# SwiGLU feed-forward: the first 256 rows of x turned by a transposing DMA copy instead of TensorE

## The chip, the cores and the metric

The kernel runs on one core of a Trainium2 chip. The metric is the device time of one execution in microseconds. Before the change it was 163.65 us, the median of 3 runs (163.2 to 164.01).

## What is computed

```python
B, S, D, F = 1, 2048, 640, 1536        # all tensors bfloat16

def reference(x, w_gate, w_up, w_down):
    g = silu(x @ w_gate)               # [S, F]
    u = x @ w_up                       # [S, F]
    return (g * u) @ w_down            # [S, D]
```

## The kernel before

All operands stay in SBUF. The 2048 rows of x are worked in four blocks of 512 (`S_BLK`). For each block and each of the twelve 128-wide slices `fc` of F, TensorE multiplies five 128x128 weight tiles (`kd`, over D = 640) with the transposed block `xT`, once for the gate (`pg`) and once for the up projection (`pu`). ACT takes silu of `pg` (L214), VectorE multiplies it with `pu` into `aT` (L215). Then the down projection goes over `aT` and `wd_sb` (L261 for the last 128 columns, L291 for the first 512), ACT copies the result out of PSUM and SP stores it. The last four rows are computed on VectorE with products and sums (`row_dots`, L147), spread over the later blocks.

The matmuls need x with D on the partitions. Rows 256 to 2047 are brought in that layout by transposing DMA copies (`turn_x`, L105), all issued from SP. Rows 0 to 255 are loaded as they lie into `x_sb` (`load_x`, L86), one 128-row chunk from SP and one from ACT; TensorE turns them with ten 128x128 transposes against the identity `ident` (`transpose_chunk`, L185), and ACT and VectorE copy the results to `xT` (L190). GpSimd makes the identity.

The start of the kernel is written out by hand. SP's queue has, in this order: the x chunk, four slices of the gate weights (`wg_sb[:, kd, 0:512]`, L115, one for each kd; the one of kd = 1 comes from ACT's queue), the transposing copy of rows 256-511, two slices of the up weights (L83), the larger weight chunks, the down weights (L125), and the transposing copy for block 1. On ACT, the first silu, which brings its table in, stands behind its two DMA issues (L119). `keep_order` holds the order of TensorE, ACT, VectorE and SP as it was traced, so that no scheduler moves these.

`head()` does the first four slices `fc` of block 0. TensorE first does `N_WARM` = 18 matmuls on ones (L176), whose result is not used, then the ten transposes, then gate steps for all four slices with kd outermost: kd = 0 in two halves of 128 columns, kd = 1 to 4 with 256 columns (rows 0-255), and then all kd with the other 256 columns (rows 256-511). The four up projections with 512 columns follow, each with its silu and product. From there on the loops are the plain ones.

Of the kernel before, what the change touches and what calls it, by code (L numbers as in the profile page):

```python
# [7 lines left out]


@with_exitstack  # L10
def _body(
# [8 lines left out]
    nc = tc.nc  # L20
    P = nc.NUM_PARTITIONS
    f32 = mybir.dt.float32
    bf16 = mybir.dt.bfloat16
    ACT = mybir.ActivationFunctionType
    ALU = mybir.AluOpType

    B, S0, D = x.shape
    F = w_gate.shape[1]
    S = B * S0
    x2 = x.rearrange("b s d -> (b s) d")  # L30
    out2 = out.rearrange("b s d -> (b s) d")

    KD = D // P
# [4 lines left out]
    HALF = S_BLK // 2  # L38
    DA = 512
    Q = 32  # L40
    N_WARM = 18
    T = 4
    WT_STEP = 4
    ROW_J = 0
    EARLY = 4
# [3 lines left out]
    consts = ctx.enter_context(tc.tile_pool(name="consts", bufs=1))  # L49
    work = ctx.enter_context(tc.tile_pool(name="work", bufs=3))  # L50
    outp = ctx.enter_context(tc.tile_pool(name="outp", bufs=3))
    psum = ctx.enter_context(
        tc.tile_pool(name="psum", bufs=2, space=bass.MemoryType.PSUM)
    )

    ident = consts.tile([P, P], bf16)
    x_sb = consts.tile([P, HALF // P, D], bf16)
    xT = consts.tile([P, KD, S], bf16)
    wg_sb = consts.tile([P, KD, F], bf16)
    wu_sb = consts.tile([P, KD, F], bf16)  # L60
# [7 lines left out]
    row_s = consts.tile([P, KF, T], f32)  # L68
    prod = consts.tile([P, D], f32)

    make_identity(nc, ident[:])

    x_v = x2.rearrange("(c p) d -> p c d", p=P)
    xt_v = x2.rearrange("s (kd p) -> s kd p", p=P)
    wg_v = w_gate.rearrange("(kd p) f -> p kd f", p=P)
    wu_v = w_up.rearrange("(kd p) f -> p kd f", p=P)
# [2 lines left out]
    def wslice(a, b):  # L79
        return slice(a * P, b * P)  # L80

    def load_w(eng, dst, src, a, b):
        eng.dma_start(out=dst[:, :, wslice(a, b)], in_=src[:, :, wslice(a, b)])  # L83

    def load_x(eng, c0, c1):
        eng.dma_start(out=x_sb[:, c0:c1, :], in_=x_v[:, c0:c1, :])  # L86

    def issue_order(a, b):
        tc.add_manual_dep(
# [8 lines left out]
    def keep_order(engine):  # L98

        traced = [i for i in nc.cur_bb.bb.instructions if i.engine == engine]  # L100
        for a, b in zip(traced, traced[1:]):
            issue_order(a, b)

    def turn_x(r0, r1):
        nc.sync.dma_start_transpose(out=xT[:, :, r0:r1], in_=xt_v[r0:r1])  # L105

    ones = consts.tile([P, P], bf16)
    silu_first = consts.tile([P, 1], f32)
    nc.vector.memset(ones[:], 1.0)  # L109

    load_x(nc.sync, 0, 1)
    load_x(nc.scalar, 1, 2)
    for kd in range(KD):
        eng = nc.scalar if kd == 1 else nc.sync
        eng.dma_start(  # L115
            out=wg_sb[:, kd, wslice(0, EARLY)], in_=wg_v[:, kd, wslice(0, EARLY)]
        )
    turn_x(HALF, S_BLK)
    nc.scalar.activation(silu_first[:], ones[:, 0:1], ACT.Silu)  # L119
    for a in range(0, EARLY, 2):  # L120
        load_w(nc.sync, wu_sb, wu_v, a, a + 2)
    for a, b in W_CHUNKS:
# [6 lines left out]
    def turn_w(dst, src, f0, f1):  # L129
# [7 lines left out]
        out=x_row[:],  # L137
        in_=x2[S - T : S, :].rearrange("t d -> (t d)").partition_broadcast(P),
# [35 lines left out]
    def warm(n):  # L174
        for _ in range(n):
            nc.tensor.matmul(  # L176
                pw[:, 0:P], lhsT=ones[:], rhs=ones[:], start=True, stop=True
            )

    def transpose_chunk(c, parts):  # L180
        c_sl = slice(c * P, (c + 1) * P)
        for copy, tag, k0, k1 in parts:
            pt = psum.tile([P, k1 - k0, P], bf16, tag=tag, name="pt")
            for kd in range(k0, k1):
                nc.tensor.transpose(  # L185
                    out=pt[:, kd - k0, :],
                    in_=x_sb[:, c, kd * P : (kd + 1) * P],
                    identity=ident[:],
                )
            copy(out=xT[:, k0:k1, c_sl], in_=pt[:])  # L190

    def proj_step(ps, w_sb, fc, sb, c0, c1, kd):
        nc.tensor.matmul(  # L193
            ps[:, c0:c1],
            lhsT=w_sb[:, kd, fc * P : (fc + 1) * P],
            rhs=xT[:, kd, sb * S_BLK + c0 : sb * S_BLK + c1],
            start=(kd == 0 and c0 in (0, HALF)),
            stop=(kd == KD - 1),
        )

    def proj(ps, w_sb, fc, sb, c0, c1):
        for kd in range(KD):
            proj_step(ps, w_sb, fc, sb, c0, c1, kd)
# [6 lines left out]
    def gate(pg, pu, sb, fc, n_s):  # L210

        s0 = sb * S_BLK
        sg = work.tile([P, S_BLK], f32, name="sg")
        nc.scalar.activation(sg[:, 0:n_s], pg[:, 0:n_s], ACT.Silu)  # L214
        nc.vector.tensor_tensor(  # L215
            out=aT[:, fc, s0 : s0 + n_s], in0=sg[:, 0:n_s], in1=pu[:, 0:n_s], op=ALU.mult
        )

    def head():
        dve, act = nc.vector.tensor_copy, nc.scalar.copy  # L220
        split = [(act, "po_a", 0, 2), (dve, "po_b", 2, KD)]
        pgs = [
            psum.tile([P, S_BLK], f32, tag="gu", name="pg", bufs=4)
            for _ in range(EARLY)
        ]
        warm(N_WARM)
        for c in range(HALF // P):
            transpose_chunk(c, split)

        steps = [(0, 0, P), (0, P, HALF)]  # L230
        steps += [(kd, 0, HALF) for kd in range(1, KD)]
        steps += [(kd, HALF, S_BLK) for kd in range(KD)]
        for kd, c0, c1 in steps:
            for fc in range(EARLY):
                proj_step(pgs[fc], wg_sb, fc, 0, c0, c1, kd)

        for fc in range(EARLY):
            pu = psum.tile([P, S_BLK], f32, tag=("po_a", "po_b")[fc % 2], name="pu")
            proj(pu, wu_sb, fc, 0, 0, S_BLK)
            gate(pgs[fc], pu, 0, fc, S_BLK)  # L240
        keep_order(mybir.EngineType.PE)
        keep_order(mybir.EngineType.Activation)

    head()
    for sb in range(NSB):
        n_s = S_BLK if sb < NSB - 1 else S_BLK - T
# [26 lines left out]
        for q in range(P // Q):  # L273
            nc.scalar.dma_start(
                out=out2[
                    sb * S_BLK : sb * S_BLK + n_t, DA + q * Q : DA + (q + 1) * Q
                ].rearrange("(i r) c -> r i c", r=Q),
                in_=ot_q[q * Q : (q + 1) * Q, :].rearrange("r (i c) -> r i c", c=Q),
            )

        for j in range(SUB):
# [6 lines left out]
            for c0, c1, tag in cols:  # L288
# [14 lines left out]
                eng = nc.sync if c1 < D else nc.scalar  # L303
# [82 lines left out]
def kernel(tc, *args):  # L386
    _body(tc, *args)
    tc.close()
    tc.compile()
    _trim(tc.nc)  # L390
# [30 lines left out]
```

## Time and profile before

| | |
|---|---|
| time, median of 3 runs | 163.65 us (163.2 to 164.01) |
| span of the profiled execution, first to last instruction | 161.8 us |
| time of the runs above that span | 1.4 to 2.2 us, 1.85 for the median |
| TensorE matmul busy | 159.4 us (99%) |
| VectorE, ACT busy | 111.0 us (69%), 42.6 us (26%) |
| DMA | 15.86 MB, mean 98 GB/s |
| transposing copies of x, from SP | 4 |

The profile is one execution; it gives the span, and the time that the runs show beyond it lies around the span. PE is TensorE's matmul side, PEld its weight load, SPq and ACTq the DMA issues of SP and ACT, L12 a line of the kernel. A matmul's length includes its way through the array, so that lengths of neighbours overlap; the distance between starts is the pace.

### The profile page before, as it was taken

To read this page: it belongs to the slowest core of one execution; us is meant where nothing else is said; L and a number is where in the kernel's file an instruction comes from. 1 tells how busy PE (TensorE), PEld (TensorE's weight loads), DVE (VectorE), ACT (ScalarE), POOL (GpSimd) and SP (SyncE) were. 2 spreads that over 40 slices of the span, in tenths; PEclk is the share of its full clock that TensorE was granted. 3 is DMA by queue.
4 is the path that set the end of the run, shared out by engine and by line. 5 is a ranking of instruction groups with operands and counts; after the bars stand their busy time and mean duration, and the time that the engine had idled before them with its cause. 6 is when DMAs were issued, how large, how long until landed. Compare 5 with 4: busy or idle time off the path is not lost.

```text
span 161.8 us, 2142 instructions
## 1 busy us (share of the span) xinstructions
PE 159.4 (99%) x808; PEld 77.6 (48%) x808; DVE 111.0 (69%) x250; ACT 42.6 (26%) x74; POOL 0.6 (0%) x6
## 2 busy tenths in 40 slices
PE   8999999999999999999999999999999999999995
PEld 7854444444444444444444444444444444445454
DVE  2034223599569999989919999979964999993001
ACT  5051222112222222211222322221214222222121
POOL 1000000000000000000000000000000000000000
PEclk9999999999999999999999999999999999999999
DMA  6999999934189999003110000000321000000312
GB/s 212 231 351 349 361 248 231 222 75 91 34 192 159 235 236 184 4 0 34 65 65 0 0 4 2 0 0 3 62 67 34 0 0 0 0 0 4 48 41 73
DMA packets 41961, 15.86 MB, mean 98 GB/s; under 512 B 33504, under 2 KB 41824, under 8 KB 41952
## 3 DMA queue, kind: packets, MB, share of 16 engines
q1 hardware_dynamic: 33584, 14.93, 37.0%
q10 hardware_dynamic: 8368, 0.80, 3.5%
q8 instruction: 6, 0.10, 0.3%
q14 instruction: 3, 0.02, 0.1%
HBM read 6.88 MB, written 2.62 MB: 59 GB/s over the span
## 4 chain that ended last, share of the span: by engine, by line
PE 97%; DMA 2%; SPq 0%; DVE 0%; issue 0%
PE pg L193 32%; PE pu L193 32%; PE po_a L291 26%; PE po_t L261 6%; DMA wg_sb<-in_w_gate_dram 2%; SPq L86 0%; DVE ot_b L302 0%
## 5 line engine op out<-in xcount | busy, mean ns | idle before, releaser
L193 PE MATMUL pg<-xT,wg_sb 128*128 128x512 bf16 (+3 forms) x264 | 59.8, 363 | 0.1
L193 PE MATMUL pu<-xT,wu_sb 128*128 128x512 bf16 (+1 forms) x240 | 59.1, 379 | 0.0
L215 DVE TENSOR_TENSOR aT<-sg,pu 128x512 bf16<-128x512 f32 (+1 forms) x48 | 32.7, 682 | 32.3 <-PE pu L193 32.3
L214 ACT ACTIVATE sg<-pg 128x512 f32<-128x512 f32 (+1 forms) x48 | 28.4, 597 | 71.2 <-PE pg L193 67.4
L291 PE MATMUL po_a<-wd_sb,aT 128*128 128x512 bf16 (+4 forms) x228 | 42.8, 348 | 0.0
L147 DVE SCALAR_TENSOR_TENSOR prod<-wgT,x_row 128x640 f32<-128x640 bf16 x48 | 39.4, 821 | 1.5 <-DMA wgT<-in_w_gate_dram 0.4
L147 DVE SCALAR_TENSOR_TENSOR prod<-wuT,x_row 128x640 f32<-128x640 bf16 x48 | 39.4, 821 | 1.0
L193 PEld LDWEIGHTS <-wg_sb 128*128 128x128 bf16 x264 | 25.9, 100 | 26.8 <-DMA wg_sb<-in_w_gate_dram 0.4
L193 PEld LDWEIGHTS <-wu_sb 128*128 128x128 bf16 x240 | 23.4, 98 | 28.1 <-DMA wu_sb<-in_w_up_dram 0.3
L291 PEld LDWEIGHTS <-aT 128*128 128x128 bf16 x228 | 20.8, 98 | 21.7
L300 ACT CAST ot<-po_a 128x512 bf16<-128x512 f32 (+2 forms) x17 | 9.5, 559 | 31.8 <-PE po_a L291 20.2
L261 PE MATMUL po_t<-aT,wd_sb 128*128 128x512 bf16 (+1 forms) x48 | 10.4, 366 | 0.0
L261 PEld LDWEIGHTS <-wd_sb 128*128 128x128 bf16 x48 | 4.7, 98 | 5.1
L302 DVE CAST ot_b<-po_a 128x96 bf16<-128x96 f32 (+1 forms) x2 | 0.5, 240 | 9.7 <-PE po_a L291 9.6
L270 ACT CAST ot_t<-po_t 128x512 bf16<-128x512 f32 (+1 forms) x4 | 2.2, 559 | 11.6 <-PE po_t L261 11.6
L147 DVE DVE_READ_ACCUMULATOR prod<-wgT,x_row 128x1 f32 x48 | 3.9, 82 | 0.0
L147 DVE DVE_READ_ACCUMULATOR prod<-wuT,x_row 128x1 f32 x48 | 3.9, 82 | 0.0
L272 DVE STREAM_TRANSPOSE ot_q<-ot_t 128x512 bf16<-128x512 bf16 (+1 forms) x4 | 2.7, 676 | 1.7 <-ACT ot_t L270 1.7
L190 DVE COPY xT<-pt 128x384 bf16<-128x384 bf16 x2 | 0.7, 358 | 2.9 <-PE pt L185 2.9
L176 PE MATMUL pw<-ones 128*128 128x128 bf16 x18 | 2.1, 313 | 0.4 <-DVE ones L109 0.4
L176 PEld LDWEIGHTS <-ones 128*128 128x128 bf16 x18 | 1.8, 147 | 0.4 <-DVE ones L109 0.4
L119 ACT ACT_TABLE_LOAD x1 | 1.3, 1283 | 1.0 <-issue 1.0
(13 smaller groups left out, 4.7 us busy)
## 6 DMA issues: line engine op xcount, KB each, us to landing
wd_sb<-in_w_down_dram SPq DMA_DIRECT2D x1, 1920.0 KB, 13.0
out_dram<-ot SPq DMA_DIRECT2D x15, 128.0 KB, 1.7
wg_sb<-in_w_gate_dram SPq DMA_DIRECT2D x2, 640.0 KB, 7.9
wu_sb<-in_w_up_dram SPq DMA_DIRECT2D x2, 640.0 KB, 8.6
wu_sb<-in_w_up_dram SPq DMA_DIRECT2D x2, 320.0 KB, 4.7
x_row<-in_x_dram SPq DMA_DIRECT2D x1, 640.0 KB, 5.1
wg_sb<-in_w_gate_dram SPq DMA_DIRECT2D x4, 128.0 KB, 3.4
out_dram<-ot_q ACTq DMA_DIRECT2D x12, 32.0 KB, 1.9
```

Of the source, the lines that this page charges most:

```text
L119: nc.scalar.activation(silu_first[:], ones[:, 0:1], ACT.Silu)
L147: nc.vector.scalar_tensor_tensor(out=prod[:], in0=wT[:, fc, :], scalar=1.0, in1=x_row[:, t, :], op0=ALU.mult, op1=ALU.mult, accum_out=acc[ ...
L176: nc.tensor.matmul(pw[:, 0:P], lhsT=ones[:], rhs=ones[:], start=True, stop=True)
L190: copy(out=xT[:, k0:k1, c_sl], in_=pt[:])
L193: nc.tensor.matmul(ps[:, c0:c1], lhsT=w_sb[:, kd, fc * P : (fc + 1) * P], rhs=xT[:, kd, sb * S_BLK + c0 : sb * S_BLK + c1], start=(kd == 0 ...
L214: nc.scalar.activation(sg[:, 0:n_s], pg[:, 0:n_s], ACT.Silu)
L215: nc.vector.tensor_tensor(out=aT[:, fc, s0 : s0 + n_s], in0=sg[:, 0:n_s], in1=pu[:, 0:n_s], op=ALU.mult)
L261: nc.tensor.matmul(po_t[:], lhsT=wd_sb[:, kf, DA:D], rhs=aT[:, kf, sb * S_BLK : sb * S_BLK + n_t], start=(kf == 0), stop=(kf == KF - 1),)
L270: nc.scalar.copy(ot_t[:], po_t[:])
L272: nc.vector.transpose(out=ot_q[:], in_=ot_t[:])
L291: nc.tensor.matmul(po[:], lhsT=aT[:, kf, s0 : s0 + P], rhs=wd_sb[:, kf, c0:c1], start=(kf == 0), stop=(kf == KF - 1),)
L300: nc.scalar.copy(ot[:], po[:])
```

## The change

Rows 0-255 of x come by the same kind of transposing copy as the others, issued from SP as its first DMA. The gate slices follow it on SP's queue as three transfers (kd 0; kd 1-2; kd 3-4), none on ACT's, then the transposing copy of rows 256-511, then all as before. `x_sb`, the identity, the ten transposes and their copies are gone. ACT begins with the first silu. There are 26 warming matmuls instead of 18, and the first gate step (kd = 0) is done in 256 columns at once, like the others.

```diff
-    N_WARM = 18
+    N_WARM = 26
...
-    ident = consts.tile([P, P], bf16)
-    x_sb = consts.tile([P, HALF // P, D], bf16)
...
-    make_identity(nc, ident[:])
...
-    load_x(nc.sync, 0, 1)
-    load_x(nc.scalar, 1, 2)
-    for kd in range(KD):
-        eng = nc.scalar if kd == 1 else nc.sync
+    def load_d(eng, k0, k1):
         eng.dma_start(
-            out=wg_sb[:, kd, wslice(0, EARLY)], in_=wg_v[:, kd, wslice(0, EARLY)]
-        )
+            out=wg_sb[:, k0:k1, wslice(0, EARLY)], in_=wg_v[:, k0:k1, wslice(0, EARLY)]
+        )
+
+    nc.scalar.activation(silu_first[:], ones[:, 0:1], ACT.Silu)
+    turn_x(0, HALF)
+    load_d(nc.sync, 0, 1)
+    load_d(nc.sync, 1, 3)
+    load_d(nc.sync, 3, KD)
     turn_x(HALF, S_BLK)
-    nc.scalar.activation(silu_first[:], ones[:, 0:1], ACT.Silu)
...
-    def transpose_chunk(c, parts):
...
-        dve, act = nc.vector.tensor_copy, nc.scalar.copy
-        split = [(act, "po_a", 0, 2), (dve, "po_b", 2, KD)]
...
         warm(N_WARM)
-        for c in range(HALF // P):
-            transpose_chunk(c, split)
-
-        steps = [(0, 0, P), (0, P, HALF)]
-        steps += [(kd, 0, HALF) for kd in range(1, KD)]
+        steps = [(kd, 0, HALF) for kd in range(KD)]
         steps += [(kd, HALF, S_BLK) for kd in range(KD)]
```

More of the change, by code (lines that the diff above doesn't have):

```diff
@@ L6 @@
 from concourse._compat import with_exitstack
-from concourse.masks import make_identity
 @with_exitstack
@@ L69, in _body @@
     prod = consts.tile([P, D], f32)
-    make_identity(nc, ident[:])
-    x_v = x2.rearrange("(c p) d -> p c d", p=P)
     xt_v = x2.rearrange("s (kd p) -> s kd p", p=P)
@@ L83, in load_w @@
         eng.dma_start(out=dst[:, :, wslice(a, b)], in_=src[:, :, wslice(a, b)])
-    def load_x(eng, c0, c1):
-        eng.dma_start(out=x_sb[:, c0:c1, :], in_=x_v[:, c0:c1, :])
     def issue_order(a, b):
@@ L178, in warm @@
             )
-    def transpose_chunk(c, parts):
[L181 to L188, printed above, removed]
-                )
-            copy(out=xT[:, k0:k1, c_sl], in_=pt[:])
     def proj_step(ps, w_sb, fc, sb, c0, c1, kd):
```

## The prediction

> **What bounds the kernel now.** I read the busy shares first, then the chain of work that ended last, then the first 16 us of the timeline, then the DMA issues with their landings.
>
> ```profile
> span 161.8 us, 2142 instructions
> PE 159.4 (99%) x808; PEld 77.6 (48%) x808; DVE 111.0 (69%) x250; ACT 42.6 (26%) x74; POOL 0.6 (0%) x6
> PE 97%; DMA 2%; SPq 0%; DVE 0%; issue 0%
> ```
>
> TensorE is the bound, and 97% of the chain is its matmuls. The chain in order of time (start, us, what) shows the only part that is not:
>
> ```profile
> 0.45 3.21 DMA wg_sb<-in_w_gate_dram
> 3.71 5.21 PE pg L193 x44
> 8.92 4.37 PE pu L193 x20
> 13.29 1.08 PE pg L193 x5
> ...
> 30.55 2.59 PE po_t L261 x12
> ```
>
> From 8.92 on, every five 512-column matmuls take 1.08 us without a gap, up to the end. Nothing behind the first up-projection changes in this edit, so the whole question is when that first pu matmul starts. A shift there goes to the end one for one, unless a load further on is late too.
>
> ```profile
> 0.00 0.39 SPq L86 DMA_DIRECT2D x_sb<-in_x_dram  x1
> ...
> 0.39 2.10 PE L176 MATMUL pw<-ones 128*128 128x128 bf16 x18 [0.39 <-DVE ones L109]
> 0.45 1.84 SPq L115 DMA_DIRECT2D wg_sb<-in_w_gate_dram  x4
> ...
> 2.31 1.25 PE L185 MATMUL pt<-ident,x_sb 128*128 128x128 bf16 x10
> ...
> 2.33 1.91 SPq L105 DMA_TRANSPOSE xT<-in_x_dram  x1
> ...
> 4.29 1.15 SPq L83 DMA_DIRECT2D wu_sb<-in_w_up_dram  x2
> ...
> 8.63 1.57 ACT L214 ACTIVATE sg<-pg 128x512 f32<-128x512 f32 x3 [4.98 <-PE pg L193]
> ...
> 8.79 4.49 PE L193 MATMUL pu<-xT,wu_sb 128*128 128x512 bf16 x20
> ```
>
> The columns are start, length, engine, line. SP's issues stand back to back: 0.46 us for each gate slice (1.84 over 4), 1.91 us for one transposing copy of 256 rows, 0.58 us for each up slice. How long from issue to landing, in the first 7 us (KB each, median us), and for the first up slice alone:
>
> ```profile
> wg_sb<-in_w_gate_dram SPq DMA_DIRECT2D x4, 128.0 KB, 3.4
> x_sb<-in_x_dram SPq DMA_DIRECT2D x1, 160.0 KB, 2.3
> xT<-in_x_dram SPq DMA_TRANSPOSE x1, 4.2
> ```
>
> ```profile
> L83 SPq DMA_DIRECT2D wu_sb<-in_w_up_dram x1: 583/583/583, 4.3 to 4.3; - x1
> DMA to landing us min/median/max: 4.5/4.5/4.5
> ```
>
> The transposed rows 256-511 land at 2.33 + 4.2 = 6.53, the first up slice at 4.29 + 4.5 = 8.79. That is exactly the start of pu. So **two transfers set the head, both on the edge**: behind 6.53 stand twenty 256-column matmuls of the second half, and pu follows 2.26 us after that landing (8.79 - 6.53); the up slice lands 2.26 us after it as well.
>
> **The change, part by part.**
>
> *TensorE.* Ten transposes (1.25 us) and their two pairs of copies go, eight warming matmuls come: 2.10 / 18 = 0.117 us each with the last one's tail, 0.107 between starts, so the warming ends near 0.39 + 26 x 0.107 = 3.2. The first eight 128-column matmuls become four of 256 columns, the same columns. All this is before the data is there, worth nothing by itself. The identity on GpSimd and the table load moved ahead on ACT are worth nothing too: ACT's first sigmoid-linear work is at 8.63.
>
> *SP's issues.* Now the queue holds: transposing copy 1 at 0.0 for 1.91; three gate transfers, the first 0.46, the two double ones between 0.46 and the 0.58 of the five-slice up load, say 0.52; then transposing copy 2. It is issued at 1.96 + 0.46 + 2 x 0.52 = 3.46, against 2.33: **1.13 us later**. The ACT queue, which carried one x chunk and one gate slice, helps no more. If copy 2 again lands 4.2 us after its issue, it lands at 7.66, +1.13: the upper bound of this chain.
>
> *The transfers themselves.* The other end comes from bytes. These are windows of the trace (busy times, then granted clock, DMA share, GB/s), and a 512-row copy, issued at 44.6 into a nearly empty queue:
>
> ```profile
> 5.10:5.80 0.70, 0.70 (x9) 0.63 (x7) 0.00 (x0) 0.00 (x0) 0.00 (x0) 1.00 1.27 275
> 5.80:6.80 1.00, 1.00 (x11) 0.81 (x10) 0.00 (x0) 0.00 (x0) 0.00 (x0) 1.00 0.52 118
> 6.80:8.80 2.00, 2.00 (x21) 1.66 (x18) 0.00 (x0) 0.17 (x1) 0.00 (x0) 1.00 1.01 308
> 45.80:46.90 1.10, 1.10 (x7) 0.50 (x6) 1.10 (x2) 0.12 (x1) 0.00 (x0) 1.00 0.87 159
> 46.90:48.50 1.60, 1.60 (x9) 0.69 (x7) 1.56 (x5) 0.47 (x1) 0.00 (x0) 1.00 1.27 286
> ```
>
> ```profile
> L105 SPq DMA_TRANSPOSE xT<-in_x_dram x1: 2732/2732/2732, 44.6 to 44.6; - x1
> DMA to landing us min/median/max: 5.4/5.4/5.4
> ```
>
> That copy began to move bytes at about 45.8, 1.2 us after its issue, went at 159 GB/s for 1.1 us and then at 286. Copy 1 is 328 kB: 1.2 + 1.1 us for the first 175 kB, 0.53 us for the other 153, so it is drained near 2.85 and lands some 0.65 later (as copy 2 now does: drained by 5.85, landed 6.53), at 3.5. Its price beside the two plain x loads is small in bytes and large in what follows: after the transposing copy of the trace, from 5.8 to 6.8, the engines moved 118 GB/s where 308 was to be had, 0.62 us lost. Now that dip comes twice, the first time ahead of the gate slices. Gate slices: 2.85 + 0.62 + 655 kB at 308 (2.1) = 5.6. Copy 2 at 286: 1.15, drained at 6.7; landing 0.65 later, **7.35, +0.8**. Without a dip behind copy 1 it would be 6.7, +0.2; that is the lower bound. I take **+0.85**, between the two chains (+0.8 by bytes, +1.13 by issue) and next to the one by bytes, since SP's 1.91 may be shorter where no earlier transfer fills the queue (half of the 2.73 for 512 rows is 1.37, which takes 0.54 off the issue chain).
>
> In the Trainium skill, Advanced Engine Details and Errata, X-Bar Transpose (TRN2), transposing copies are as fast as plain ones, 350 to 400 GB/s. The windows above differ: 159 and then 286 GB/s, and the measurement decides; by the page's figure copy 1 would drain about 0.7 us sooner and the sum would be near +0.15.
>
> *The first gate matmuls* wait for copy 1 (3.5) and for gate slice 0, which stands behind it: 2.85 + 0.62 + 131 kB at 308 (0.43) + about 0.5 to land = 4.4 (bounds: 1.96 + 2.3 = 4.3 by the quick x load, 1.96 + 3.4 = 5.4 by the slow gate loads). So TensorE starts pg 0.7 us later than 3.71 and idles 1.2 us instead of 0.4. The first half, 20 matmuls of 256 columns, needs 2.2 us at the pace of the second half and so ends at 6.6 to 6.9, ahead of 7.4: hidden, as long as the pace is that. If it is not, see the clock below.
>
> *The up slices* follow copy 2 on the queue, 2.26 us behind its landing as now, so they come when pu wants them. The load one chunk further has this much room:
>
> ```profile
> 10.11 1.67 SPq L125 DMA_DIRECT2D wd_sb<-in_w_down_dram  x1
> ...
> 14.06 0.89 PEld L193 LDWEIGHTS <-wu_sb 128*128 128x128 bf16 x5 [0.19 <-DMA wu_sb<-in_w_up_dram]
> 14.20 1.24 PE L193 MATMUL pu<-xT,wu_sb 128*128 128x512 bf16 x5
> ```
>
> ```profile
> wd_sb<-in_w_down_dram SPq DMA_DIRECT2D x1, 1920.0 KB, 13.0
> ```
>
> Between the weight load and its matmul stand 0.14 us. If the stream moves by 1.13 and TensorE by 0.85, 0.14 more is lost there; the range has it. The down weights land at 23.1 and are first used at 30.55, so they have room.
>
> **Sum:** 161.8 + 0.85 = 162.65 of span. The runs of before lie 1.4 to 2.2 us above that span (163.2 to 164.01), 1.85 for the median, so 164.5 against 163.65.
>
> **Rivals.**
>
> *The clock (slower still).* The granted-clock column says 1.00 from the start, but the spacing says otherwise:
>
> ```profile
> 3.71 0.72 PE L193 MATMUL pg<-xT,wg_sb 128*128 128x128 bf16 x5
> 6.27 2.65 PE L193 MATMUL pg<-xT,wg_sb 128*128 128x256 bf16 x22
> 1.54:4.95 3.41, 3.26 (x29) 2.81 (x28) 0.72 (x2) 1.71 (x4) 0.00 (x0) 1.00 0.96 287
> ```
>
> 128 columns took (0.72 - 0.29) / 4 = 0.107 us until then; later 256 columns take (2.65 - 0.27) / 21 = 0.113, a stall included. TensorE ran at half speed up to about 4.95, 4.5 us of almost unbroken work. Now the work breaks off from 3.2 to 4.4. If the count starts anew there, the whole first half runs at 0.214 each, 4.4 + 4.3 = 8.7, the second takes 2.2 and a little more: pu at 11.0, +2.2. If it changes at 7.0: 12 done by then, 8 at 0.11, 7.9 + 2.2 = 10.1, +1.3. So 165.0 to 165.9, middle 165.4. For it: the break, and that a faster TensorE would starve between gate slices. Against: the trace has a break of 0.4 us in its stretch and still got full speed at 4.95. The Trainium skill, TensorE: Matmul & The Clock Gate, Part 1, has a free-running window of about 3.4 us which must be busy; an estimate from it: a warming of 2.8 us does not fill one, which speaks against this change. The trace's 3.26 busy of 3.41 agrees with it but does not show how much idleness is allowed.
>
> *Hidden anyway (no change).* No dip behind copy 1, SP's issue 1.37: copy 2 lands at 6.7, +0.2, 163.85. For it: two issues fewer on ACT's queue, whose packets shared the same engines. Against: the 118 GB/s.
>
> *Faster.* The gate slices now have one queue, and the first copy drains before them. If copy 1 is through by 2.6 and the slices need only 1.87 us (350 GB/s), copy 2 drains at 5.6 and lands at 6.25, and pu starts 0.3 us sooner: 163.35. It decides in favour when copy 2 lands ahead of 6.53. Against: copy 2 cannot be issued before 2.9 even with 1.37 for the first, and every dip must be gone.
>
> That the change does not do what it says is out: the instruction order has the two transposing copies first and fifth on SP and no transposes on TensorE.
>
> **How the numbers follow.** A measurement of this kernel tells about 0.5% (0.82 us) from no change. Forecast 164.5 (164.2 to 164.8): 0.48, of which 0.29 lies over 164.47. Clock: 0.27, all slower. Hidden: 0.18, same. Faster: 0.07, of which 0.05 is allowed beyond 0.5%. Slower 0.29 + 0.27 = 0.56, same 0.39, faster 0.05. The range goes from 163.5, which takes in most of the hidden case, to 165.9, the end of the clock's; it leaves out the faster case and the lower edge of the hidden one, under 2 in 10.
>
> **What would show it.** In the changed profile: copy 1 issued at 0.0 for 1.4 to 1.9 us and landing near 3.5; pg's first matmul near 4.4 with a wait of over 1 us on a gate slice, not on xT; copy 2 issued near 3.5, landing near 7.4; a low-rate stretch after each copy; pu at 9.65; from there the same 1.08 us steps. Wrong if pu starts under 9.0 (the dip or the issue was overpriced), or over 10, with 256-column matmuls 0.214 apart beyond 6 us (the clock).

## The result and the profile after

| | before | after |
|---|---|---|
| time, median of 6 runs | 163.64 us | 165.58 us (164.74 to 165.86) |
| ratio after / before | | 1.0118, 95% interval 1.0096 to 1.0141 |
| span of the profiled execution | 161.8 us | 164.5 us (a run of 165.86 us) |

The change costs 1.94 us, at the median. The two profiled executions differ by 2.7 us, since that of before was one of the quick ones: this run of after lies 1.36 us above its span, and the profiled runs below lie 1.3 above theirs, so a span of 161.8 belongs to some 163.15 us, not to the median.

The chain of work that ended last, in order of time, for the first 18 us of the kernel after (start, us, what):

```profile
0.00 1.34 SPq L96
1.34 0.06 issue
1.39 0.56 SPq L103
1.96 0.05 issue
2.01 3.88 DMA wg_sb<-in_w_gate_dram
5.89 0.05 issue
5.93 5.77 PE pg L174 x36
11.70 0.05 issue
11.76 4.26 PE pu L174 x19
```

The DMA piece is the second gate transfer (kd 1-2), which stands behind slice 0 on the queue: it landed at 2.01 + 3.88 = 5.89, and 36 of the 40 gate matmuls come behind it. The gate matmuls end, by their modelled ends, at 11.70 instead of 8.92. (The record of the first pu matmul is missing; 19 of 20 are there. Before, it started 0.13 us ahead of that modelled end, which puts it near 11.55 here, against 8.79.) Behind them the steps are the old 1.08 us. The timeline of the same execution:

```profile
0.39 2.96 PE L169 MATMUL pw<-ones 128*128 128x128 bf16 x26 [0.39 <-DVE ones L100]
1.39 1.55 SPq L103 DMA_DIRECT2D wg_sb<-in_w_gate_dram  x3
2.98 2.28 SPq L96 DMA_TRANSPOSE xT<-in_x_dram  x1
5.22 6.49 PE L174 MATMUL pg<-xT,wg_sb 128*128 128x256 bf16 x40 [1.87 <-DMA wg_sb<-in_w_gate_dram]
```

TensorE stands idle from the end of its warming to 5.22, and what it waits for is a gate slice, not x; behind the first four gate matmuls comes a second, shorter break, up to 5.93. Issue and landing of the first copy (L96), the first gate slice (L103) and the second copy (L96):

```profile
L96 SPq DMA_TRANSPOSE xT<-in_x_dram x1: 1336/1336/1336, 0.0 to 0.0; - x1
DMA to landing us min/median/max: 3.7/3.7/3.7
...
L103 SPq DMA_DIRECT2D wg_sb<-in_w_gate_dram x1: 563/563/563, 1.4 to 1.4; - x1
DMA to landing us min/median/max: 3.8/3.8/3.8
...
L96 SPq DMA_TRANSPOSE xT<-in_x_dram x1: 2279/2279/2279, 3.0 to 3.0; - x1
DMA to landing us min/median/max: 4.9/4.9/4.9
```

Copy 1 lands at 3.7, gate slice 0 at 1.39 + 3.8 = 5.2, copy 2 at 2.98 + 4.9 = 7.9. That is 1.36 later than before, and if that were all, pu would start 2.26 behind it, at 10.1. It starts near 11.55. The rest is in the granted clock. These are four stretches of the kernel after (busy times by engine; the last three columns are granted clock, DMA share, GB/s):

```profile
0.39:3.33 2.94, 2.94 (x26) 2.69 (x26) 0.00 (x0) 1.22 (x2) 0.04 (x2) 1.00 0.61 128
3.33:6.74 3.41, 1.43 (x13) 1.04 (x13) 0.00 (x0) 0.00 (x0) 0.00 (x0) 1.00 1.03 245
6.74:10.15 3.41, 3.41 (x19) 2.43 (x17) 0.00 (x0) 0.00 (x0) 0.00 (x0) 0.50 1.06 274
10.15:11.54 1.39, 1.39 (x14) 1.25 (x13) 0.00 (x0) 0.13 (x1) 0.00 (x0) 1.00 1.04 344
```

The clock column reads 1.00 until the first change that was recorded, at 3.33; the 26 warming matmuls before it are 0.107 us apart, which the prediction showed to be half the pace. From 3.33 on the full clock was granted. TensorE was busy for 1.43 us of the stretch 3.33 to 6.74, and in the next one, of the same 3.41 us, it was granted half the clock. Its matmuls, in the timeline by shape:

```profile
6.71 3.58 PE L174 MATMUL pg<-xT,wg_sb 128*128 128x256 bf16 x16
```

Sixteen in 3.58 us with the last one's tail, over 0.2 us apart where 0.11 is the full pace. The full clock had come early, while there was nothing to multiply; twelve gate matmuls ran at it, and then it was gone for the next sixteen. The Trainium skill, TensorE: Matmul & The Clock Gate, Part 1, tells of a free-running window of about 3.4 us and of two clocks, full and half; the stretches of this trace agree (3.41, 1.00 and 0.50). It lets the clock fall after an idle window; here a stretch with 1.43 us of work was idle enough, and the measurement decides. Where the stretches fall is not the same in every execution: e3 below has the same warming and a like break, and its clock rose at 8.70, so that its gate began at half speed.

### The profile page after: what moved, and what is told of

Read it like the earlier page. It is cut to its first block, busy times and chain, and to the rows that moved or that the text cites. A ratio compares the mean times of both kernels' runs of the same rounds, so it can differ in the third digit from the quotient of the medians.

```text
span 164.5 us, 2106 instructions
## 1 busy us (share of the span) xinstructions
PE 159.7 (97%) x790; PEld 77.8 (47%) x802; DVE 110.4 (67%) x248; ACT 41.9 (25%) x72; POOL 0.2 (0%) x4
## 4 chain that ended last, share of the span: by engine, by line
PE 95%; DMA 2%; SPq 1%; issue 0%; DVE 0%
PE pg L174 32%; PE pu L174 31%; PE po_a L266 26%; PE po_t L236 6%; DMA wg_sb<-in_w_gate_dram 2%; SPq L96 1%; SPq L103 0%; DVE ot_b L277 0%
## 5 line engine op out<-in xcount | busy, mean ns | idle before, releaser
L174 PE MATMUL pg<-xT,wg_sb 128*128 128x512 bf16 (+2 forms) x254 | 60.6, 371 | 2.3 <-DMA wg_sb<-in_w_gate_dram 1.9
L169 PE MATMUL pw<-ones 128*128 128x128 bf16 x26 | 3.0, 313 | 0.4 <-DVE ones L100 0.4
L169 PEld LDWEIGHTS <-ones 128*128 128x128 bf16 x26 | 2.7, 148 | 0.4 <-DVE ones L100 0.4
```

The source lines that it names most:

```text
L169: nc.tensor.matmul(pw[:, 0:P], lhsT=ones[:], rhs=ones[:], start=True, stop=True)
L174: nc.tensor.matmul(ps[:, c0:c1], lhsT=w_sb[:, kd, fc * P : (fc + 1) * P], rhs=xT[:, kd, sb * S_BLK + c0 : sb * S_BLK + c1], start=(kd == 0 ...
```

## Experiments

Ratios are to the kernel before on the same chip, with 95% intervals. Two theories: the **clock theory**, that the break in TensorE's work costs most of what copy 2's landing does not explain; and the **transfer theory**, that the late landings alone make the 1.9 us. Then, what makes the landings late.

### Longer warming (e1), hardly any (e9)

```diff
-    N_WARM = 26
+    N_WARM = 60      # e9: 1
```

> The changed kernel with 60 warming matmuls instead of 26, so that TensorE is busy until the first gate slice lands near 5.2. Clock theory (the break from 3.2 to 5.2 lets TensorE fall back to half speed from 6.7 to 10.2, worth some 1.4 us in the profiled run): no half-speed stretch behind 5.5, time near 164.5 to 164.9, 0.7 to 1.1 us under the changed kernel's 165.6 and 0.9 to 1.3 over before. Transfer theory (the late landings alone make the 1.9 us): no change, 165.6. If the longer warming itself delays the first gate matmul by more than the break, over 165.6.

> The changed kernel with 1 warming matmul instead of 26, so that TensorE is all but idle until the first gate slice lands near 5.2. If the loss is a matter of stretches of 3.4 us, each of which grants the next one its speed by how busy it was, the warming buys a full-speed stretch while TensorE has nothing to do: without it the gate runs at half speed from 5.2 to somewhere between 7 and 11, and the time is 165.2 to 166.4, no better and on the mean no worse than 165.6. If the warming itself caused the drop by coming too early: under 165.0. Transfer theory: 165.6 unchanged.

Measured: 60 matmuls 164.72 us (1.0066, 1.0044 to 1.0087), 26 are the change itself (1.0118), 1 gives 165.74 us (1.0149, 1.0124 to 1.0174). The same stretches with 60, and the gate's rows in the timelines of both, first 60, then 1:

```profile
3.33:6.74 3.41, 3.41 (x46) 3.30 (x44) 0.00 (x0) 0.00 (x0) 0.00 (x0) 1.00 1.01 247
6.74:10.15 3.41, 3.41 (x32) 2.97 (x31) 0.00 (x0) 0.19 (x1) 0.00 (x0) 1.00 1.11 279
```

```profile
5.63 4.63 PE L174 MATMUL pg<-xT,wg_sb 128*128 128x256 bf16 x40
```

```profile
4.74 7.47 PE L174 MATMUL pg<-xT,wg_sb 128*128 128x256 bf16 x40 [4.05 <-DMA wg_sb<-in_w_gate_dram]
```

With 60 there is no break and the 40 matmuls take 4.63 us, although they begin 0.4 later than in the change; without warming they take 7.47. (The clock column is of no use in these two executions, since no change was recorded in them: with 1 warming matmul it reads 1.00 also where the matmuls are 0.21 us apart.) The copies land where they did (copy 2 at 7.9 with 60, at 7.5 with 1). So the transfer theory falls: with 60 the landings stayed and the time fell by 0.85 us, 1.94 to 1.1, with intervals apart. Some 0.85 us is what the longer warming brings back by the clock, and 1.1 is the rest; since 60 warming matmuls ended 0.5 after the gate slice's landing, 1.1 is rather too much for the landings alone, and 0.85 too little for the clock. Whether the 26 were worth anything against 1 is not settled, the intervals of 1.0118 and 1.0149 just overlap.

### No warming in the kernel before (e2)

```diff
-    N_WARM = 18
+    N_WARM = 1
```

> The kernel before with 1 warming matmul instead of 18: no transfer changes, only TensorE's early work is missing until 2.3 us. Clock theory: full speed comes later, the first half of the gate is slower, 0.5 to 1.5 us over before (164.1 to 165.1). Transfer theory: the two transfers at 6.5 and 8.8 set the time whatever the speed is, so no change (within 0.3 us).

Measured: 163.98 us, 1.0017 (0.9995 to 1.0040): no difference that can be told, as the transfer theory had it for this kernel. Its timeline says why:

```profile
2.59 1.25 PE L185 MATMUL pt<-ident,x_sb 128*128 128x128 bf16 x10 [1.91 <-DMA x_sb<-in_x_dram]
3.63 3.19 PE L193 MATMUL pg<-xT,wg_sb 128*128 128x128 bf16 x24
7.12 2.34 PE L193 MATMUL pg<-xT,wg_sb 128*128 128x256 bf16 x20 [0.30 <-DMA xT<-in_x_dram]
```

From 2.59 TensorE has work without a long break, the first half of the gate is done by 6.8, and copy 2 (7.1 in this execution) sets the rest. The kernel before owes its steady work to the early x chunks, not to the warming. It also shows that copy 2's landing varies by half a microsecond between two executions with the same transfers (6.53 and 7.1).

### Gate slices from ACT's queue (e3)

```diff
-    load_d(nc.sync, 0, 1)
-    load_d(nc.sync, 1, 3)
-    load_d(nc.sync, 3, KD)
+    load_d(nc.scalar, 0, 1)
+    load_d(nc.scalar, 1, 3)
+    load_d(nc.scalar, 3, KD)
```

ACT's first silu stands behind the three issues here.

> The changed kernel with the three gate transfers issued from ACT's queue, so that they do not stand behind the first transposing copy and the second copy is issued at about 1.4 instead of 3.0. If the queue order is what makes the gate slices and the second copy late: gate slice 0 lands before 4.2, the second copy before 6.8, time within 0.4 us of before (163.2 to 164.0). If it is the transposing copies themselves (slow stretches, shared engines) and not the order: second copy still near 7.5 and time 164.5 or more.

Measured: 165.72 us, 1.0129 (1.0112 to 1.0145). The two copies (L96), and the stretch in which the gate matmuls begin:

```profile
L96 SPq DMA_TRANSPOSE xT<-in_x_dram x1: 1322/1322/1322, 0.0 to 0.0; - x1
DMA to landing us min/median/max: 5.6/5.6/5.6
...
L96 SPq DMA_TRANSPOSE xT<-in_x_dram x1: 2141/2141/2141, 1.4 to 1.4; - x1
DMA to landing us min/median/max: 6.2/6.2/6.2
```

```profile
5.29:8.70 3.41, 3.03 (x15) 2.17 (x15) 0.00 (x0) 0.00 (x0) 0.00 (x0) 1.00 1.22 252
```

The gate slices no longer stand behind copy 1, and now copy 1 lands at 5.6, with the traffic of the other queue beside it. Copy 2, issued 1.6 us sooner than in the change, lands at 7.6, 0.3 sooner. So its issue time is not what sets its landing. The break in TensorE's work is as long as ever (2.32 us), only it now ends with copy 1, at 5.6, and the first 15 gate matmuls take 3.03 us, 0.2 us each, up to the rise of the clock at 8.70 (until which the clock column reads 1.00).

### A plain copy in the place of the first transposing one (e4, e13)

```diff
-    turn_x(0, HALF)
+    nc.sync.dma_start(
+        out=xT[:, :, 0:HALF],
+        in_=x2[0:HALF].rearrange("(p r) d -> p (r d)", p=P).rearrange(
+            "p (kd s) -> p kd s", s=HALF
+        ),
+    )
```

> The changed kernel with the first transposing copy replaced by a plain copy of the same bytes in the same place of SP's queue; the 256 rows are not transposed, so their results are not the reference's. It prices the crossbar: by the theory that the transposing copy costs a slow start and a slow stretch behind it (1.5 us against 0.9 for its bytes, then 0.6), gate slice 0 lands 0.8 to 1.3 us sooner (3.9 to 4.4), the second copy near 6.9, time 164.0 to 164.6. If the order on one queue is what costs, not the crossbar: gate slice 0 still lands near 5 and the time stays over 165.

e13 is the same with 60 warming matmuls.

> The changed kernel with 60 warming matmuls and a plain copy of the same bytes in the place of the first transposing copy (rows 0-255 are not transposed, so their results are not the reference's). If the crossbar makes what the queue order does not (0.4 us): 164.2 to 164.4. If the place on one queue makes it all: 164.6 to 164.9, as with the transposing copy and long warming.

Measured: e4 165.50 us (1.0092, 1.0067 to 1.0117), e13 164.84 us (1.0065, 1.0042 to 1.0089). Gate slice 0, copy 2 and the later gate matmuls in e4, and the GB/s of e4 where the change has its slow stretch:

```profile
L103 SPq DMA_DIRECT2D wg_sb<-in_w_gate_dram x1: 608/608/608, 0.7 to 0.7; - x1
DMA to landing us min/median/max: 3.3/3.3/3.3
...
L96 SPq DMA_TRANSPOSE xT<-in_x_dram x1: 1807/1807/1807, 2.4 to 2.4; - x1
DMA to landing us min/median/max: 5.7/5.7/5.7
```

```profile
6.02 5.77 PE L179 MATMUL pg<-xT,wg_sb 128*128 128x256 bf16 x36 [1.30 <-DMA wg_sb<-in_w_gate_dram]
```

```profile
3.00:3.50 0.50, 0.35 (x4) 0.08 (x1) 0.00 (x0) 0.00 (x0) 0.00 (x0) 1.00 1.25 228
3.50:4.00 0.50, 0.00 (x0) 0.00 (x0) 0.00 (x0) 0.00 (x0) 0.00 (x0) 1.00 0.61 168
4.00:4.50 0.50, 0.39 (x4) 0.31 (x4) 0.00 (x0) 0.00 (x0) 0.00 (x0) 1.00 0.72 197
4.50:5.00 0.50, 0.22 (x2) 0.00 (x0) 0.00 (x0) 0.00 (x0) 0.00 (x0) 1.00 0.88 258
```

and the same stretches of the change:

```profile
3.00:3.50 0.50, 0.35 (x4) 0.08 (x1) 0.00 (x0) 0.00 (x0) 0.00 (x0) 1.00 0.62 118
3.50:4.00 0.50, 0.00 (x0) 0.00 (x0) 0.00 (x0) 0.00 (x0) 0.00 (x0) 1.00 0.77 176
4.00:4.50 0.50, 0.00 (x0) 0.00 (x0) 0.00 (x0) 0.00 (x0) 0.00 (x0) 1.00 0.91 244
4.50:5.00 0.50, 0.00 (x0) 0.00 (x0) 0.00 (x0) 0.00 (x0) 0.00 (x0) 1.00 1.03 364
```

Half of the expectation came: gate slice 0 lands at 4.05 instead of 5.2. But the engines then move 168 to 258 GB/s without any transposing copy in front, copy 2 is issued 0.6 us sooner and lands at 2.36 + 5.7, near 8.0, not sooner at all. The second gate transfer, through which the chain goes here as in the change, is there at 5.97 instead of 5.89, so the early slice 0 only moves the break behind the first four matmuls. With long warming the plain copy gives 1.0065 against the transposing one's 1.0066, and its copy 2 lands at 8.2. So the transposing in the first copy is not what makes the transfers behind it late; that the place in the queue is, is tried next. (The time of e13 says less than its landings: in its profiled execution the chain went through the 60 warming matmuls, which ended at about 6.2, so a gain of 0.2 us at the landings would not have been seen.)

### Parts of the queue order in the kernel before (e5, e6, e11)

```diff
 # e5: three gate transfers, all from SP
-    for kd in range(KD):
-        eng = nc.scalar if kd == 1 else nc.sync
-        eng.dma_start(
-            out=wg_sb[:, kd, wslice(0, EARLY)], in_=wg_v[:, kd, wslice(0, EARLY)]
-        )
+    for k0, k1 in ((0, 1), (1, 3), (3, KD)):
+        nc.sync.dma_start(
+            out=wg_sb[:, k0:k1, wslice(0, EARLY)], in_=wg_v[:, k0:k1, wslice(0, EARLY)]
+        )
 # e6: five gate transfers and both x chunks, all from SP
-    load_x(nc.scalar, 1, 2)
+    load_x(nc.sync, 1, 2)
-        eng = nc.scalar if kd == 1 else nc.sync
+        eng = nc.sync
 # e11: e5, and both x chunks from SP
```

> The kernel before with its gate slices as three transfers from SP (kd 0; 1-2; 3-4), the x chunks and TensorE's transposes as they were. If the larger transfers and the loss of ACT's help for one slice are what makes the copy of rows 256-511 late: it lands at 7.4 or later and the time is 0.5 to 1 us over before (164.2 to 164.7). If the place of the first transposing copy is the cause: it lands at 6.5 to 7.1 as before and the time is within 0.3 us.

> The kernel before with both x chunks and all five gate slices from SP, none from ACT. If one queue instead of two is what costs (slow start, issues one behind the other): the second copy, issued at about 3.3, lands near 7.5 to 7.9 and the time is 0.6 to 1.2 us over before. If the queue does not matter: landing at 6.5 to 7.1 and no change.

> The kernel before with all of SP's part of the change except the transposing copy: both x chunks and three gate transfers from SP's queue, rows 0-255 still turned on TensorE. If the queue order makes most of the transfers' loss: second copy lands near 7.5, 164.2 to 164.6, near the 164.7 of the changed kernel with long warming. If the first transposing copy makes it: within 0.3 us of before.

Measured: e5 163.91 us (1.0025, 0.9998 to 1.0051), e6 164.18 us (1.0041, 1.0023 to 1.0058), e11 163.89 us (1.0040, 1.0011 to 1.0069). Copy 2 in e5 and in e6:

```profile
L105 SPq DMA_TRANSPOSE xT<-in_x_dram x1: 2350/2350/2350, 1.9 to 1.9; - x1
DMA to landing us min/median/max: 5.4/5.4/5.4
```

```profile
L105 SPq DMA_TRANSPOSE xT<-in_x_dram x1: 1820/1820/1820, 3.3 to 3.3; - x1
DMA to landing us min/median/max: 4.3/4.3/4.3
```

Issued 1.4 us apart, they land 0.3 apart, at 7.3 and 7.6. All of the start on SP's queue, with TensorE's transposes kept, costs about 0.65 us by the ratios of e6 and e11; three gate transfers from SP alone (e5) cost 0.4 us by the ratio, and the interval reaches to none. The 0.65 is over half of the 1.1 us which the change costs with a steady clock, but it is loose. e11, the nearest to the change, has seven times from 163.6 to 163.9 and five from 164.6 to 165.7: its median is 0.29 us above the kernel before, which is what was expected if the first transposing copy were the cause, and its interval reaches from 0.2 to 1.1 us. The other 0.4 us lies within the intervals of e1 and e11.

### Three orders that were to better it (e7, e8, e10) and the opposite change (e12)

All but e12 start from the change with 60 warming matmuls. e7 has five gate slices from SP; e8 issues gate slice 0 ahead of copy 1; e10 has five slices, that of kd 1 from ACT. e12 is the kernel before with ten more transposes on TensorE for rows 256-511 and no transposing copy in the head.

```diff
 # e7
-    load_d(nc.sync, 0, 1)
-    load_d(nc.sync, 1, 3)
-    load_d(nc.sync, 3, KD)
+    for kd in range(KD):
+        load_d(nc.sync, kd, kd + 1)
 # e8
-    turn_x(0, HALF)
     load_d(nc.sync, 0, 1)
+    turn_x(0, HALF)
 # e10
+    load_d(nc.scalar, 1, 2)
...
+    for kd in (0, 2, 3, 4):
+        load_d(nc.sync, kd, kd + 1)
 # e12, in head(), before the last gate step of rows 0-255
+            if kd == KD - 1 and c0 == 0:
+                for c in range(HALF // P, S_BLK // P):
+                    transpose_chunk(c, split)
...
-    turn_x(HALF, S_BLK)
+    load_x(nc.sync, 2, 4)
```

> The changed kernel with 60 warming matmuls (so that the clock does not disturb, 164.7) and the gate slices as five transfers, all from SP. If the double slices are what makes the engines end apart: gate slice 0 and the second copy land sooner by 0.3 us or more, 164.0 to 164.4. If not: two issues more put the second copy about 0.5 us later, 164.9 to 165.2.

> The changed kernel with 60 warming matmuls and gate slice 0 issued ahead of the first transposing copy. If a plain transfer pays for standing behind a transposing copy (its engines end 1.2 us apart): gate slice 0 lands near 2.5 and the first gate matmul is free at the first copy's landing, near 4.3; the second copy keeps its place near 7.9, so the time stays at 164.7. A time under 164.3 would say that the order of the first two sets the second copy's landing too.

> The changed kernel with 60 warming matmuls, the gate slices as five transfers and the one of kd 1 from ACT, as before. If the loss of ACT's queue is what the transfers lost: the second copy lands at 7.4 or earlier, 164.0 to 164.4. If traffic on a second queue holds back the first transposing copy, as when all gate slices came from ACT: first copy lands after 4.5, second near 7.9, 164.7 or more.

> The opposite of the change: rows 256-511, too, come by a plain load in the second copy's place on SP and are turned on TensorE, ten more transposes between the gate steps of rows 0-255. If the wait for the second copy's landing (6.5 to 7.1 before) sets the time: pu starts sooner by up to 0.5 us, 163.1 to 163.6. If the ten transposes (0.6 to 1.1 us) and their copies cost more than the wait: 164.0 to 164.6.

Measured: e7 165.81 us (1.0126, 1.0057 to 1.0196), e8 164.92 us (1.0084, 1.0052 to 1.0116), e10 164.83 us (1.0075, 1.0058 to 1.0091), e12 164.73 us (1.0076, 1.0061 to 1.0091). None is under e1, and none beats the kernel before. e7 is inconclusive: its interval is wide, and its profiled execution waited for late up weights as well. In e8 the gate slice is there at 2.1 and copy 1 only at 4.2; copy 2 lands at 8.0. The times of the three say little about the landings, though, since the chain goes through the warming in all of them: with 60 matmuls the first gate matmul began at 5.63 in e1, 5.80 in e8, 6.09 in e7 and 6.49 in e10, by how soon the clock rose (in e1 the warming matmuls go from 0.107 to 0.056 us apart near 4.4, in e10 near 6.2). In e10 copy 1 landed at 3.5 and copy 2 at 3.42 + 4.2 = 7.6, neither as expected, and the gate, which ran without a wait from 6.49 to pu at 10.86, could not have shown a gain of that. Whether that order is better with a warming that ends sooner was not tried. In e12 the wait moved to the plain load:

```profile
6.96 0.73 PE L185 MATMUL pt<-ident,x_sb 128*128 128x128 bf16 x10 [1.09 <-DMA x_sb<-in_x_dram]
7.53 2.80 PE L193 MATMUL pg<-xT,wg_sb 128*128 128x256 bf16 x24
```

It landed (2.3 + 4.6 = 6.9) between the two landings seen of the transposing copy in its place (6.53 and 7.1), and the transposes came on top.

## Why the prediction was wrong

The direction and the range held; the forecast of +0.85 us was less than half of the 1.94.

- *"hidden, as long as the pace is that"* is the step that failed. The first half of the gate was put at full speed, done by 6.9 and hidden behind copy 2. TensorE had lost its clock at 6.74 and finished the gate near 11.55. The rival with the clock, given 0.27 and 165.0 to 165.9, is what happened, and e1 shows it; the sign that was named for it, pu over 10 with matmuls 0.214 apart beyond 6 us, is in the trace. Its pu, at 10.1 to 11.0, was still too early for the 11.55, since the gate data came later than it had them (5.2 and 5.9 against 4.4). Its mechanism, too, was a little different from "the count starts anew": full speed had come at 3.33, was spent on waiting, and was taken back after a stretch with too little work. In e3's execution it went as the rival said, half speed from the first gate matmul up to 8.70.
- *Gate slice 0* was put at 4.4 with 5.4 as the upper bound; it landed at 5.2. This made the break 2 us instead of 1.2, and it is the break that decided. The gate transfer behind it (kd 1-2) was given no landing of its own in the prediction; it came at 5.89 and held back the other 36 gate matmuls.
- *Copy 2* was put at 7.4, between 6.7 and an upper bound of 7.66. It was issued at 2.98, not at 3.46, and landed at 7.9 all the same. The bound by issue (issue + 4.2) was no bound: issues from 1.37 (e3) to 2.98 (the change) gave landings of 7.6, 7.3 (e5), 8.0 (e4) and 7.9, so that the time from issue to landing is not fixed: 6.2, 5.4, 5.7 and 4.9 us.
- *The dip behind copy 1* was there (118 GB/s from 3.0 to 3.5), but e4 has such a stretch with a plain copy (168 GB/s from 3.5 to 4.0), and its copy 2 lands no sooner. So the dip is not the price of transposing. Copy 1's own landing, 3.5 forecast and 3.7 measured, was right.
- *The transfers' share*, +0.85, measured 1.1 with a steady clock (e1: 0.7 to 1.4): right within its interval, and with long warming, which adds something of its own. About 0.65 of it is the queue order by the ratios of e6 and e11, of which e11's reaches from 0.2 to 1.1. What makes the rest, if it is there at all, stays open.
- *"worth nothing by itself"* for the warming: not so where the warming closes the break, since 34 matmuls more brought 0.85 us back (e1). The eight more of the change were not tried alone.
- *The sum's base:* 1.85 us was put between span and median; the profiled runs show 1.3, so the execution of before was half a microsecond quicker than its median.
- *Hidden* and *faster* needed copy 2 at 6.7 or under 6.53; it was at 7.9. Nothing further on was late: pu moved by about 2.75 us and the span by 2.7.

## What to carry to other kernels

When an edit opens a pause in TensorE's early work, price the clock beside the wait: cut the time into stretches, add up the busy time in each, and look at the clock granted in the next. Warming that ends before the data lands can be worth little; it should reach to the landing, and not beyond it, where it holds up the work itself (e10). And when one transfer is put ahead of others on a queue, follow the last of them: the time from issue to landing of a transfer that stands behind others is not a property of that transfer.

## What was not expected of the hardware

- How much work a stretch of 3.41 us needs was not the same at both clocks, as far as these few go. At the full clock, 1.43 us of matmuls (the change) and 1.45 us (e4, 3.45 to 6.86) were followed by half of it, and 2.31 us (e12, 3.50 to 6.91) by the full one again. At half the clock, 2.63 us (e9, 3.96 to 7.37, counted back from 10.78, where its matmuls go from 0.21 to 0.11 us apart) were followed by half, and 2.96 us (e4, 0.04 to 3.45) by the full one.
- A transposing copy beside traffic from another queue landed at 5.6 us (e3); ahead of the same traffic on its own queue, at 3.7; and with only one gate slice on the other queue, at 3.5 (e10).
- SP spent 1.34 us on issuing the copy of 256 rows as its first transfer and 2.28 us on the second of the same shape, so 1.91 was not its fixed price.
